# Attention, a dense expert and a soft mixture of experts on one core: another order of the first part

## The chip, the cores and the metric

The kernel is one program on one core of a Trainium2 chip. The metric is the time of one execution on the device in microseconds (us). The kernel before takes 650.18 us, the median of 3 runs (649.59 to 650.78).

## The reference, cut to what matters

Three parts follow each other: attention over chunks of 32 tokens with memory tokens, a dense layer with a squared ReLU, and a soft mixture of 8 experts. The change lies in the first two, where the attention of the first block of tokens and the first steps of the dense layer overlap.

```
for c in range(nc):                       # attention, chunk by chunk
    scores = scale * np.matmul(q_c, k_full.transpose(0, 1, 3, 2))
    scores = scores - np.max(scores, axis=-1, keepdims=True)
    a = np.exp(scores)
    a = a / (np.sum(a, axis=-1, keepdims=True) + 1e-09)
    out[:, :, c_start:c_end] = np.matmul(a, v_full)
...
h = x @ w_in                              # dense layer, 512 -> 2048 -> 512
r = np.maximum(h, 0.0)
g = s * (r * r) + b
return (g @ w_out).astype(np.float32)
...                                       # then the soft mixture on its result
```

## The kernel before, in words

The 3072 tokens are handled in 6 blocks of 512. In a block, the attention works on 4 pairs of heads, called units; the dense layer walks over 16 slices of 128 hidden columns, called steps. Blocks of the first pass are u = 0 to 3, the second block's are u = 4 to 7. Products in full precision are made of three fast matmuls: every operand is split into a high part and a low part, and high x high, high x low and low x high are summed. The weights of the dense layer arrive as raw 64-bit numbers and have to be turned into 32-bit floats first, half a slice at a time.

What is done, and by which engine, in the letters of the order that is written out by hand in the string FIRST (a letter and a number; the number is the unit, the step or the half slice):

- S and s spread q (L205, L207); B the scores on TensorE (L220); a the row maximum and the subtraction on VectorE (L234, L235); b the exponential on ScalarE (L239); f the sums and their reciprocals on VectorE (L247 to L249); j the scaling on GpSimd (L253).
- U is four transposes of a unit's probabilities on TensorE (L263). The result is copied into a block layout in two halves, p for the first (ScalarE, L273) and C for the second (VectorE, L275, or ScalarE, L273, by a list of units in the step table). V is the product with the values on TensorE (L285), u the copy of the high part of x on ScalarE (L292), X the low part of x on VectorE (L308).
- w loads half slices of weights into free staging tiles (L320, SyncE). d clamps (L326, VectorE for the halves 0 and 1, GpSimd for the others), e and h are the high and the low word (L330, L335, ScalarE), E merges them into the weight (L340, VectorE) and gives the staging tile back.
- I and i are the high and the low part of the first weight of a step (L347 ScalarE; L351 VectorE or GpSimd, by a list in wi_low), O and o those of the second weight (L362, L366).
- M is a step's first product, four quarters of three matmuls, one quarter for each unit's x (L377). For step 0 the quarters stand alone: H0 to H3. R is the ReLU (L381, ScalarE), t the square (L385, VectorE), g and l the high and low part of the result (L388 ScalarE, L392 VectorE). Y is the second product, 12 matmuls (L407).
- z is a group of multiplications of zeros that keeps TensorE busy (L1239), y puts six tiles into the list of staging tiles.

Every engine takes its own part of this order strictly one after the other, and waits by semaphore for what it reads and for buffers that must be free. H0 to H3 add into one bank of PSUM, which R0 reads when all four are done. M1 adds into another bank.

Of the kernel before, what the change touches and what calls it, by code (L numbers as in the profile page):

```python
# [12 lines left out]
ALU = mybir.AluOpType  # L13
# [4 lines left out]
NF = 16  # L18
# [7 lines left out]
KG = 40  # L26
KW = CB * KG + 24
FIRST = (
# [25 lines left out]
def tile_attention_moe_softmoe(  # L54
# [13 lines left out]
    pe, act, dve, pool, sp = nc.tensor, nc.scalar, nc.vector, nc.gpsimd, nc.sync  # L68
# [82 lines left out]
    def r32(ap):  # L151
        return ap.bitcast(F32R)
# [4 lines left out]
    def hl(t):  # L157
        return t.rearrange("p (a n) -> p a n", a=2)
# [10 lines left out]
    def qv(u):  # L169
        return Q[u % 2].rearrange("p (c h n) -> p c h n", h=2, c=CB)  # L170
# [12 lines left out]
    def pbv(u):  # L183
        return PB[u % 2].rearrange("p (i a h z n) -> p i a h z n", i=4, a=2, h=2, z=2)
# [84 lines left out]
    def att_half(u, b, z, fast=True):  # L269
        src = b.rearrange("p (i a h n) -> p i a h n", i=4, a=2, h=2)[64 * z:64 * z + 64]  # L270
        dst = pbv(u)[64 * z:64 * z + 64, :, :, :, z, :]
        if fast:
            act.activation(out=dst, in_=src, func=AF.Copy)  # L273
        else:
            dve.tensor_copy(dst, src)  # L275
# [12 lines left out]
    def att_copy(u, b):  # L288
        j, hp = jh(u)
        xt = hl(X[j % 2][hp])  # L290
        if j < NPL:
            act.activation(out=r32(xt[:, 0]), in_=b, func=AF.Copy)  # L292
        else:
            act.activation(out=xraw(j, hp), in_=b, func=AF.Copy)
# [53 lines left out]

    def wi_low(n):
        t, raw = hl(WI[n % 2]), W[n % NF][:, 0:512]  # L350
        (dve if n < NF and n not in (0,) else pool).tensor_tensor(out=r32(t[:, 1]), in0=raw, in1=t[:, 0], op=ALU.subtract)  # L351

    def split_wi(n):
        wi_high(n)
        wi_low(n)
# [869 lines left out]
    with tc.manual_schedule(engines={mybir.EngineType.PE, mybir.EngineType.SP}):  # L1225
# [15 lines left out]
        for i in range(2):  # L1241
            t = qv(i)
            pool.memset(t[0:64, :, 1, :], 0.0)
            pool.memset(t[64:128, :, 0, :], 0.0)
        for i in range(2):
            t = pbv(i)
# [3 lines left out]
        sbk = {}  # L1250
# [3 lines left out]
        def took(u, b=None):  # L1254
# [15 lines left out]
            "E": w_end,  # L1270
            "I": wi_high,
            "i": wi_low,
            "H": lambda kt: mm_h(0, (kt,)),
            "R": make_r,
# [13 lines left out]
            "f": att_sum,  # L1288
            "j": lambda u: att_mul(u, pool),
            "p": lambda u: att_half(u, sbk[u], 0),  # L1290
            "C": lambda u: att_half(u, sbk[u], 1, u in (0,)),
            "u": lambda u: att_copy(u, sbk[u]),
            "X": lambda u: att_low(u, sbk[u]),
            "Z": w_store,
# [330 lines left out]
```

## Time and profile before

| | |
|---|---|
| median of 3 runs | 650.18 us (649.59 to 650.78) |
| the profiled execution | 650.11 us, of which 648.3 us are the span that the profile shows |
| TensorE busy | 636.6 us (98%), 4965 matmuls |
| VectorE, ScalarE, GpSimd busy | 438.1, 352.7 and 272.5 us |
| mean granted clock of TensorE | 0.997 of full speed |

The profile is one execution. Times in it count from its first instruction. PE is TensorE, DVE is VectorE, ACT is ScalarE, POOL is GpSimd, SP is SyncE. A row of a timeline gives start, duration, engine, line, operation, result and operands; in brackets stands how long the engine was idle before it, and who ended that. Instructions that follow each other on an engine overlap somewhat, so the distance from one start to the next, here called a slot, is shorter than a duration. TensorE's clock has two levels: a granted clock of 1.00 is 2.4 GHz, 0.50 is 1.2 GHz.

### The profile page before, as it was taken

The numbers are of one execution on the slowest core, as the hardware profiler recorded it, in microseconds if no ns is written. First come the engines' busy times: TensorE is split into PE (matmuls) and PEld (weight loads), VectorE is DVE, ScalarE is ACT, GpSimd is POOL, SyncE is SP. The second block draws the span as 40 slices with busy tenths as digits, with TensorE's granted clock in tenths as the row PEclk, the third lists the DMA queues.
The fourth block names the chain that finished last, engine by engine and source line by source line (L and its number), as shares of the span: only waits on it lengthen the run. The fifth ranks groups of instructions, "written<-read, shape, count | busy, mean of one in ns | idle before, by whom it ended". The sixth has DMA issues, their size and how long they took to land.

```text
span 648.3 us, 12864 instructions
## 1 busy us (share of the span) xinstructions
PE 636.6 (98%) x4965; PEld 511.4 (79%) x4965; DVE 438.1 (68%) x716; ACT 352.7 (54%) x632; POOL 272.5 (42%) x219
## 2 busy tenths in 40 slices
PE   8999999999999999999999999999999999999995
PEld 7788888888878888888788887888887888886384
DVE  6999989666864678656566586616766879666233
ACT  5898787655555556554344555425644456454232
POOL 5897856343343584543534102454455516000000
PEclk9999999999999999999999999999999999999998
DMA  9998854576746755978854696469999789999998
GB/s 335 406 405 304 308 193 167 175 274 234 271 166 221 277 208 211 329 259 297 293 186 178 216 332 197 182 216 355 329 352 317 240 294 328 390 391 409 406 408 317
DMA packets 60109, 184.38 MB, mean 284 GB/s; under 512 B 6672, under 2 KB 6928, under 8 KB 60048
## 3 DMA queue, kind: packets, MB, share of 16 engines
q1 hardware_dynamic: 60048, 183.56, 77.7%
q8 instruction: 39, 0.64, 0.4%
q14 instruction: 22, 0.18, 0.1%
HBM read 137.40 MB, written 46.14 MB: 283 GB/s over the span
## 4 chain that ended last, share of the span: by engine, by line
PE 94%; DVE 2%; DMA 2%; ACT 1%; issue 0%; DVEq 0%; POOL 0%; SPq 0%; ACTq 0%; POOLq 0%
PE bank L407 28%; PE bank L737 24%; PE bank L377 13%; PE bank L995 12%; PE bank L285 3%; PE bank L220 3%; PE bank L1439 2%; PE bank L459 2%; PE bank L263 2%; PE bank L1480 1%; DMA out<-x03n 1%; PE bank L433 1%; PE bank L475 1%; DMA out<-epn 1%; PE bank L1239 1%; PE bank L513 0%
## 5 line engine op out<-in xcount | busy, mean ns | idle before, releaser
L407 PE MATMUL bank<-g,wo 128*128 128x512 f32 x528 | 130.0, 395 | 0.0
L407 PEld LDWEIGHTS bank<-g,wo 128*128 128x128 f32 x528 | 96.9, 188 | 21.7 <-ACT wi L347 0.8
L377 PE MATMUL bank<-x,wi 128*128 128x512 f32 x384 | 92.7, 390 | 0.0
L377 PEld LDWEIGHTS bank<-x,wi 128*128 128x128 f32 x384 | 71.8, 188 | 15.3 <-DVE x L308 0.4
L385 DVE SCALAR_TENSOR_TENSOR rt<-bank,cons,rt 128x512 f32<-128x512 f32 x32 | 23.9, 746 | 29.1 <-ACT rt L381 28.9
L326 POOL TENSOR_SCALAR sp<-sp 128x512 f32<-128x512 f32 x20 | 43.0, 2176 | 0.0
L366 POOL TENSOR_TENSOR wo<-w,wo 128x512 fp32r<-128x512 f32 x16 | 21.9, 1367 | 45.6 <-ACT wo L362 37.0
L729 POOL TENSOR_TENSOR w14n<-sp6n,w14n 128x512 fp32r<-128x512 f32 x8 | 14.5, 1815 | 46.9 <-ACT w14n L728 46.9
L351 POOL TENSOR_TENSOR wi<-w,wi 128x512 fp32r<-128x512 f32 x17 | 22.4, 1317 | 24.6 <-ACT wi L347 21.5
L347 ACT ACTIVATE wi<-w 128x512 fp32r<-128x512 f32 x32 | 20.1, 629 | 19.6 <-PE bank L377 14.8
L392 DVE SCALAR_TENSOR_TENSOR g<-rt,cons,g 128x512 fp32r<-128x512 f32 x32 | 25.6, 799 | 6.2 <-ACT g L388 5.9
L362 ACT ACTIVATE wo<-w 128x512 fp32r<-128x512 f32 x32 | 20.1, 628 | 16.8 <-PE bank L407 8.5
L285 PEld LDWEIGHTS bank<-pb,v 128*64 128x64 f32 x704 | 22.2, 138 | 8.0 <-issue 2.5
L388 ACT ACTIVATE g<-rt,cons 128x512 fp32r<-128x512 f32 x32 | 23.1, 722 | 9.0 <-DVE rt L385 8.7
L239 ACT ACTIVATE ep<-ep 128x512 f32<-128x512 f32 x22 | 13.9, 632 | 22.8 <-DVE ep L235 22.7
L285 PE MATMUL bank<-pb,v 128*64 128x64 f32 x704 | 25.1, 225 | 0.8 <-ACT pb L273 0.5
L220 PE MATMUL bank<-k,q 128*64 128x64 f32 x704 | 24.6, 225 | 0.3 <-DMA k<-kd 0.3
L752 ACT ACTIVATE rt1n<-y1n 128x1024 f32<-128x1024 f32 x8 | 8.5, 1058 | 29.0 <-DVE y1n L854 29.0
L220 PEld LDWEIGHTS bank<-k,q 128*64 128x64 f32 x704 | 22.6, 140 | 1.7 <-issue 1.3
L381 ACT ACTIVATE rt<-bank 128x512 f32<-128x512 f32 x32 | 18.7, 584 | 6.2 <-PE bank L377 6.1
L985 POOL TENSOR_TENSOR k0n<-sp5n,k0n 128x512 fp32r<-128x512 f32 x6 | 8.2, 1360 | 32.1 <-ACT k0n L984 32.1
L247 DVE TENSOR_REDUCE ast<-ep 128x8 f32<-128x512 f32 x22 | 15.0, 681 | 8.6 <-ACT ep L239 8.2
(688 smaller groups left out, 1727.5 us busy)
## 6 DMA issues: line engine op xcount, KB each, us to landing
v<-vd SPq DMA_DIRECT2D x22, 512.0 KB, 5.2
sp<-wd SPq DMA_DIRECT2D x22, 512.0 KB, 9.4
q<-qd SPq DMA_DIRECT2D x20, 512.0 KB, 7.5
dws<-wo SPq DMA_DIRECT2D x16, 512.0 KB, 6.2
k<-kd SPq DMA_DIRECT2D x22, 332.0 KB, 6.8
wo<-dws SPq DMA_DIRECT2D x12, 512.0 KB, 5.0
dwi<-w SPq DMA_DIRECT2D x16, 256.0 KB, 6.8
dwr<-w SPq DMA_DIRECT2D x16, 256.0 KB, 6.6
```

The costliest lines, as they stand in the source:

```text
L220: pe.matmul(S[64 * par:64 * par + 64, 2 * i + z, :], lhsT=qt[:, c].rearrange("p h n -> p (h n)"), rhs=kt[:, KG * c:KG * c + 64], start=Tru ...
L285: pe.matmul(b[64 * h:64 * h + 64, 64 * m:64 * m + 64], lhsT=vt[:, m, h, :], rhs=pb[:, m // 2, m % 2, h].rearrange("p z n -> p (z n)"), sta ...
L326: eng.tensor_scalar(out=hv, in0=hv, scalar1=-EXP_TOP, scalar2=EXP_TOP, op0=ALU.max, op1=ALU.min)
L351: (dve if n < NF and n not in (0,) else pool).tensor_tensor(out=r32(t[:, 1]), in0=raw, in1=t[:, 0], op=ALU.subtract)
L366: (dve if n < NF else pool).tensor_tensor(out=r32(t[:, :, 1]), in0=raw, in1=t[:, :, 0], op=ALU.subtract)
L377: pe.matmul(HB[n % 2], lhsT=r32(w[:, a, kt, :]), rhs=r32(x[:, b]), start=(kt == 0 and i == 0), stop=(kt == 3 and i == 2))
L385: dve.scalar_tensor_tensor(out=t, in0=HB[n % 2], scalar=s_col, in1=r, op0=ALU.mult, op1=ALU.mult)
L388: act.activation(out=r32(hl(G[n % 2])[:, 0]), in_=hl(RT[n % 2])[:, 1], func=AF.Identity, bias=b_col)
L392: dve.scalar_tensor_tensor(out=r32(g[:, 1]), in0=t, scalar=b_col, in1=g[:, 0], op0=ALU.add, op1=ALU.subtract)
L407: pe.matmul(yb[dt], lhsT=r32(w[:, dt // 2, a, dt % 2 * 128:dt % 2 * 128 + 128]), rhs=r32(g[:, b]), start=(first and i == 0), stop=(last an ...
L737: pe.matmul(b, lhsT=r32(wv[:, a, kt, :]), rhs=r32(xv[:, c]), start=(first and kt == 0 and i == 0), stop=(kt == 1 and i == 2), skip_group_c ...
L995: pe.matmul(banks[d], lhsT=r32(w[:, a, d * 128:d * 128 + 128]), rhs=r32(g[:, b]), start=(first and i == 0), stop=(last and i == 2), skip_g ...
```

## The change

The string FIRST is rewritten in its first five lines: the same 475 entries, some at other places. In the step table the list of units whose second copy is made by ScalarE grows from unit 0 to units 0, 1 and 3. In wi_low the low part for step 3 goes from VectorE to GpSimd. Nothing else is changed, and nothing that is computed.

```diff
 FIRST = (
...
-    "I1 e2 H3 i1 M1 E2 R0 d4 h3 t0 w1 O0 g0 o0 e3 d5 l0 Y0 R1 E3 h4 t1 w1 I2 d6 e4 i2 g1 E4 M2 h5 l1 w1 "
...
+    "v4 v5 X3 e2 i1 E2 M1 h3 H3 R0 t0 w1 d6 O0 g0 o0 e3 l0 h4 Y0 E3 R1 w1 I2 t1 e4 g1 h5 i2 E4 M2 l1 w1 "
...
     def wi_low(n):
         t, raw = hl(WI[n % 2]), W[n % NF][:, 0:512]
-        (dve if n < NF and n not in (0,) else pool).tensor_tensor(out=r32(t[:, 1]), in0=raw, in1=t[:, 0], op=ALU.subtract)
+        (dve if n < NF and n not in (0, 3) else pool).tensor_tensor(out=r32(t[:, 1]), in0=raw, in1=t[:, 0], op=ALU.subtract)
...
             "p": lambda u: att_half(u, sbk[u], 0),
-            "C": lambda u: att_half(u, sbk[u], 1, u in (0,)),
+            "C": lambda u: att_half(u, sbk[u], 1, u in (0, 1, 3)),
```

On TensorE the place is the end of the first block's attention and the first products of the dense layer. bank_195 takes H0 to H3, bank_196 takes M1; x_87 to x_90 are the four quarters of x; the row of pb_106 with yt_108 is V3, and the row of L407 is the start of Y0.

```order
 L377 MATMUL bank_195<-x_87,wi_83 128x512 x3
 L285 MATMUL bank_191<-pb_106,yt_108 64x64 x16
+L377 MATMUL bank_195<-x_89,wi_83 128x512 x3
 L377 MATMUL bank_195<-x_88,wi_83 128x512 x3
-L377 MATMUL bank_195<-x_89,wi_83 128x512 x3
-L377 MATMUL bank_195<-x_90,wi_83 128x512 x3
 L377 MATMUL bank_196<-x_87,wi_84 128x512 x3
 L377 MATMUL bank_196<-x_88,wi_84 128x512 x3
 L377 MATMUL bank_196<-x_89,wi_84 128x512 x3
 L377 MATMUL bank_196<-x_90,wi_84 128x512 x3
+L377 MATMUL bank_195<-x_90,wi_83 128x512 x3
 L407 MATMUL bank_191<-g_95,wo_85 128x512
```

H2 stands before H1, and H3 stands behind all of M1, directly in front of Y0. Ahead of that place, two of the multiplications of zeros have moved from before U0 to behind it.

On VectorE the place is the stretch from the end of the sums of the first block (RECIPROCAL) to the low parts of x. The copies of pb_106 are C1 and C3, the one of pb_105 is C2; w_67 is the merge E0, sp_113 the clamp d1.

```order
 L249 RECIPROCAL ast_188<-ast_188 128x8
-L275 COPY pb_106<-bank_192 64x16x32
 L340 SCALAR_TENSOR_TENSOR w_67<-sp_112 128x512
 L275 COPY pb_105<-bank_193 64x16x32
+L326 TENSOR_SCALAR sp_113<-sp_113 128x512
 L308 TENSOR_TENSOR x_87<-bank_191,x_87 128x512
-L326 TENSOR_SCALAR sp_113<-sp_113 128x512
-L275 COPY pb_106<-bank_197 64x16x32
 L308 TENSOR_TENSOR x_88<-bank_194,x_88 128x512
```

C1 and C3 are gone from VectorE, and d1 stands before X0 in place of behind it.

On ScalarE the place is the same stretch, from the copies of the last unit on. The copies of pb_106 are p3 and, new, C3; x_89 and x_90 are u2 and u3; L335 is the low word h, L330 the high word e, and wi_84 is I1.

```order
 L273 ACTIVATE pb_106<-bank_197 64x16x32
 L335 ACTIVATE sp_113<-sp_113 128x512
+L273 ACTIVATE pb_106<-bank_197 64x16x32
 L292 ACTIVATE x_89<-bank_198 128x512
 L330 ACTIVATE sp_113<-sp_113 128x512
+L292 ACTIVATE x_90<-bank_191 128x512
 L335 ACTIVATE sp_114<-sp_114 128x512
-L292 ACTIVATE x_90<-bank_191 128x512
 L347 ACTIVATE wi_84<-w_68 128x512
```

C3 stands between h1 and u2, and u3 stands before h2. C1 has come in further ahead, behind e0 (not shown). On GpSimd, i3 stands behind the clamp d8, which now comes before d7. Since E1 now comes after y0, its staging tile is loaded again as the fourth of a group and not as the second.

## Rows read from the trace of the kernel before

**Rows 1.** The page: costliest groups, busy us, mean ns, then idle before them

```profile
L407 PE MATMUL bank<-g,wo 128*128 128x512 f32 x528 | 130.0, 395 | 0.0
...
L377 PE MATMUL bank<-x,wi 128*128 128x512 f32 x384 | 92.7, 390 | 0.0
```

**Rows 2.** The chain of waits, 17 to 40 us: start, us, what

```profile
21.39 0.70 DVE pb L275
...
22.14 1.15 PE bank L285 x32
23.29 5.22 PE bank L377 x21
...
31.30 2.72 PE bank L377 x12
```

**Rows 3.** Timeline of VectorE, 10 to 80 us: C1, E0, d1, E1, i1, t0

```profile
17.34 0.69 DVE L275 COPY pb<-bank 64x512 f32<-64x512 f32 x1
18.06 0.98 DVE L340 SCALAR_TENSOR_TENSOR w<-sp 128x512 uint32<-128x512 uint32 x1
...
20.41 0.95 DVE L326 TENSOR_SCALAR sp<-sp 128x512 f32<-128x512 f32 x1
...
23.32 1.05 DVE L340 SCALAR_TENSOR_TENSOR w<-sp 128x512 uint32<-128x512 uint32 x1
...
25.07 0.69 DVE L351 TENSOR_TENSOR wi<-w,wi 128x512 fp32r<-128x512 f32 x1
...
26.74 0.74 DVE L385 SCALAR_TENSOR_TENSOR rt<-bank,cons,rt 128x512 f32<-128x512 f32 x1
```

**Rows 4.** Timeline of ScalarE: e0, p2, p3, h1, u2, e1, u3, R0, g0, I3

```profile
16.48 0.66 ACT L330 ACTIVATE sp<-sp 128x512 f32<-128x512 f32 x1
17.85 0.59 ACT L273 ACTIVATE pb<-bank 64x512 f32<-64x512 f32 x1 [0.71 <-PE bank L263]
...
20.09 0.58 ACT L273 ACTIVATE pb<-bank 64x512 f32<-64x512 f32 x1
20.57 0.67 ACT L335 ACTIVATE sp<-sp 128x512 uint32<-128x512 uint8 x1
21.13 0.57 ACT L292 ACTIVATE x<-bank 128x512 fp32r<-128x512 f32 x1
21.61 0.63 ACT L330 ACTIVATE sp<-sp 128x512 f32<-128x512 f32 x1
...
23.34 0.60 ACT L292 ACTIVATE x<-bank 128x512 fp32r<-128x512 f32 x1 [0.52 <-PE bank L285]
...
25.80 0.60 ACT L381 ACTIVATE rt<-bank 128x512 f32<-128x512 f32 x1 [0.19 <-PE bank L377]
...
27.51 0.72 ACT L388 ACTIVATE g<-rt,cons 128x512 fp32r<-128x512 f32 x1
...
34.38 0.61 ACT L347 ACTIVATE wi<-w 128x512 fp32r<-128x512 f32 x1
```

**Rows 5.** Timeline of GpSimd: j3 and i0

```profile
17.45 1.04 POOL L253 TENSOR_TENSOR rt<-rt,ast 128x512 f32<-128x512 f32 x1 [0.41 <-DVE ast L249]
19.78 1.29 POOL L351 TENSOR_TENSOR wi<-w,wi 128x512 fp32r<-128x512 f32 x1 [1.29 <-ACT wi L347]
```

**Rows 6.** Timeline of TensorE: keep-warm passes at the start and later, and U2

```profile
1.31 3.79 PE L1239 MATMUL bank<-w 128*128 128x128 f32 x16 [1.31 <-POOL w L1235]
...
12.50 1.06 PE L1239 MATMUL bank<-w 128*128 128x128 f32 x8
...
17.09 0.65 PE L263 MATMUL bank<-cons,rt 128*128 128x128 f32 x4 [0.17 <-POOL rt L253]
```

**Rows 7.** Transfers issued from 8.4 to 8.8 us: KB, us to landing

```profile
sp<-wd SPq DMA_DIRECT2D x1, 512.0 KB, 10.5
```

**Rows 8.** Stretches at the end: us, busy PE, PEld, DVE, ACT, POOL, granted clock, DMA, GB/s

```profile
642.00:643.00 1.00, 0.23 (x1) 0.00 (x0) 1.00 (x3) 0.67 (x2) 0.00 (x0) 1.00 0.74 293
643.00:644.00 1.00, 0.00 (x0) 0.00 (x0) 0.21 (x1) 0.00 (x0) 0.00 (x0) 1.00 1.00 381
644.00:645.00 1.00, 0.00 (x0) 0.00 (x0) 0.00 (x0) 0.00 (x0) 0.00 (x0) 0.61 1.00 383
```

8 rows, old and new, of the table FIRST are left out of this document.

## The prediction

> **What bounds the kernel now.** I read the costliest groups of the page first. The two big matmul groups, L407 with 528 and L377 with 384 instructions, show 0.0 us of idle time in front of them [rows 1]. From its first full product on, TensorE therefore waits for nobody, and whatever moves the start of that stream moves the end by the same amount. I then followed the chain of waits through the stretch in which the stream begins [rows 2]. Before 22.14 us the chain runs on VectorE, whose last link is the copy L275 of the fourth head pair's probabilities (21.39 us, 0.70). From 22.14 on every link is TensorE: the value product V3 (1.15 us), then one piece of 21 matmuls (5.22 us) that contains H1, H2, H3 and M1, and then blocks of 12 in 2.72 us, or 0.227 us for one matmul. The third view is the timelines of the engines in that stretch [rows 3 to 6]: they give what one instruction takes, the distance from one start to the next on ScalarE, and how long a result of TensorE needs before ScalarE starts on it.
>
> One more thing has to be seen there. The first Y product needs R0, t0 and g0 in a row, and R0 needs all four quarter products H0 to H3. R0 starts at 25.80, t0 at 26.74, g0 at 27.51 and ends at 28.23 [rows 3, 4]. TensorE spends just that time on the 12 matmuls of M1 (12 x 0.227 = 2.72 us), so the latency is covered. The cover is M1, and it works only because M1 stands behind H3.
>
> **The change part by part.**
>
> *Two probability copies go to ScalarE.* VectorE loses two copies of 0.70 us [rows 2, 3]. ScalarE takes each in a form of 0.59 us (17.85) whose slot costs 0.48, by the starts 20.09 and 20.57 [rows 4]. C1 follows the exponent step at 16.48, which takes 0.66, so it ends near 17.7 and V1 starts there; with V3's 1.15 us as its length it ends at 18.85. U3 comes next, 0.65 us by the row at 17.09 [rows 6], and its result reaches ScalarE 0.76 us after its start (17.09 to 17.85) [rows 4, 6], which is 19.6. ScalarE then does p3 (slot 0.48), h1 (slot 0.56, from 20.57 to 21.13) and C3 (0.59): C3 ends near 21.2, and V3 starts at 21.25. Before it was 22.14, so this part brings 0.9 us at V3.
>
> *The clamp and the merge.* The clamp d1 moves ahead of X0 on VectorE. Its data is issued at 8.41 us and lands 10.5 us later [rows 7], at 18.9, about when the copy C2 is done, so no new wait is expected of it. It took 0.95 us beside GpSimd's subtraction at 19.78 [rows 3, 5]. Even at that price X0 is done before 21, and V3 behind it still waits for C3. The merge E1 (1.05 us at 23.32 [rows 3]) needs e1. With u2 in the slot behind C3 (21.1) and e1 0.48 later for 0.63 us [rows 4], E1 runs from about 22.4 to 23.4. Because E1 frees its staging tile after the other tiles are listed, SyncE fetches that tile as the fourth of a group and not as the second. I cost this at nothing: GpSimd's queue of clamps lies between landing and use. Were that cover gone, it would be one clamp late, in a part of the program with no idle in front of TensorE.
>
> *Keep-warm multiplications.* Two move behind U0. TensorE waits there for others anyway; cost 0.
>
> *i3 to GpSimd.* The subtraction takes 1.29 us there (19.78) in place of 0.69 (25.07) [rows 3, 5]. I3 starts at 34.38 [rows 4]; with the delay of R0 found below (2.2 us) its 0.61 us ends at 37.2, and i3 at 38.5. M3 is three blocks after Y0, and its third matmul, the first one that needs i3, comes at about 30.2 + 3 x 2.72 + 0.45 = 38.8. So it is hidden by 0.3 us. Without that cover the cost would be about 0.3 us, and at least 0.
>
> *The quarter products.* This is the term that decides. The order is now H2, H1, M1, H3.
> First M1 has to start. V3 at 21.25 gives u3 at 22.45 (1.20 us, from 22.14 to 23.34 [rows 2, 4]); u3 holds a slot of 0.48 and h2 one of 0.56: I1 starts at 23.5 and ends at 24.1; i1 (0.69) ends at 24.8. H2 and H1 are done by 23.8. The third matmul of M1 needs i1, so from 24.85 on 10 matmuls of M1 and the 3 of H3 are left: 13 x 0.227 = 2.95 us, to 27.8. The last one, 0.39 us long [rows 1], ends near 28.0.
> Then nothing is left for TensorE to do. R0 runs 28.0 to 28.6 (0.60), t0 to 29.37 (0.74 and 0.03 between engines), g0 to 30.12 (0.72 and 0.03). Y0 cannot start before, where g0 ended at 28.23. That is 1.9 us later, with TensorE idle for almost 2.4 us, in spite of the 0.9 us won at V3.
>
> **Bounds.** Above: E0 now starts at 17.34, where C1 stood, just ahead of j3 on GpSimd (17.45, 1.04 us) [rows 3, 5]. E0 took 0.98 us beside the end of j3, so the two hinder each other. If j3 is the one that waits, and for the whole of E0, it ends at 19.4 in place of 18.5, U3 and all behind it come 0.5 late, and the sum is 2.4 us. The Trainium skill, "SBUF — State Buffer", section "Who interferes with whom", says that VectorE with two SBUF inputs and a GpSimd instruction that reads SBUF take a shared pair of ports in turn, the first of them for its whole instruction; by that rule j3 is held, and the sum is the 2.4 of the bound in place of 1.9. The trace agrees at d1 (20.41 to 21.36), which ends 0.29 us after GpSimd's 19.78 + 1.29 = 21.07, and shows no case with VectorE first. Below: if no wait at all were left behind U2 (17.09), TensorE's own work would be two transposes (1.30), three value products (3.45) and 24 matmuls (5.45), ending at 27.3; R0, t0, g0 with their handovers add 2.15, and Y0 starts near 29.5, 1.2 us later than the g0 end of before allowed. I take 2.0, since the steps on ScalarE are rows in the same order and only j3 is open. 650.11 us, of which 648.3 are span, become 652.1; the median of the runs shown, 650.18, becomes 652.2.
>
> **Rivals.**
> The gap also costs clock. In the last microseconds TensorE does its last 0.23 us of work after 642.00, and the granted clock is still 1.00 (2.4 GHz) in 643 and 0.61 on average in the microsecond from 644 [rows 8]: it fell to the 1.2 GHz level some 2 us after the last matmul. A gap of 2.4 us, with another short wait for i1 shortly ahead, is of that size; against it speaks that TensorE is much busier before this gap than in the tail. The price from rows: at the start 16 warm-up passes took 3.79 us, where 8 later took 1.06, so 16 should take 2.12; 1.67 us were lost in a slow stretch [rows 6]. Part of such a stretch would fall into the gap itself, so I take 1.5 on top of 2.0: 653.7. The Trainium skill, "TensorE: Matmul & The Clock Gate", section "HAM oscillation — how this bites in real kernels", warns of just this, idle gaps that put the engine back to the lower clock so that the next products start slow; the tail agrees with it, and no gap of this size in the middle of this trace tests it.
>
> Everything keeps up. If the copies on ScalarE free the start of the stream so far that I1 and i1 are no longer waited for, only the bound below is left, 1.2 us, and 651.4 is no measurable change. For it speaks that VectorE is the chain up to V3 and gets lighter. Against it speaks that V3 still waits for C3, now behind U3, p3 and h1 on ScalarE, and M1 for I1. It decides from the point where V3 starts before about 20.6.
>
> The other side: the delay is given back, as other engines gain 2 us of lead on TensorE and later waits vanish, and with V3 0.9 us earlier the kernel gets faster by some of that, at most 649.3. Against it: there are no waits of TensorE in front of the two large groups to be saved [rows 1]. It would need H3 to be done by 25.8 us as before, which 24.85 for i1 excludes.
>
> **How the numbers follow.** What a measurement of this kernel can tell from no change is about 0.2%, 1.3 us. Chances: forecast 0.58, with its own range 651.6 to 652.9; clock as well 0.27; everything keeps up 0.11; given back 0.04. The first two are slower, 0.85; the third is the same, 0.11; the last is faster, 0.04. The range, 651.2 to 654.2, takes in the bound below at one end and the clock at the other.
>
> **What would show it.** Right: in the profile after, V3 near 21.3; TensorE's block at L407 first starts near 30.2, with an idle time of more than 2 us in front of it that ends with ScalarE's L388; L381 first starts near 28.0; and from then on the stream has the shift of 2 us up to the end. The copies L275 at C1 and C3 stand on ScalarE in slots of 0.48. The clock rival shows as a granted clock under 1.00 around 28 to 34 us and matmuls of twice 0.227. Wrong: an L407 that starts before 29.6, or a shift at the end that differs from that at 30 us by more than 0.5.

## The result, and the profile after

The changed kernel takes 655.94 us, the median of 5 runs (655.55 to 656.24); the kernel before takes 650.18 (649.59 to 650.79, 5 runs). The ratio is 1.0082, with a 95% interval of 1.0071 to 1.0092: slower by 5.8 us, where 2.0 were forecast and 654.2 was the upper end of the range. The profiled execution took 655.63 us, of which 653.8 are the span: 5.5 more than before.

On the page, the group L407 now has idle time in front of it, where it had none [rows 1]. Columns as there.

```profile
L407 PE MATMUL bank<-g,wo 128*128 128x512 f32 x528 | 131.6, 399 | 3.0 <-ACT g L388 3.0
...
L377 PE MATMUL bank<-x,wi 128*128 128x512 f32 x384 | 93.4, 391 | 0.5 <-DVE x L308 0.3
```

The timeline of TensorE shows where these 3.0 us stand: one gap of 2.28 us in front of Y0, as forecast, and a second one of 0.72 us at 84 us, which nothing in the forecast explains.

```profile
21.17 0.73 PE L377 MATMUL bank<-x,wi 128*128 128x512 f32 x2 [0.32 <-DVE x L308]
21.84 1.15 PE L285 MATMUL bank<-pb,yt 128*64 128x64 f32 x32
...
24.76 3.97 PE L377 MATMUL bank<-x,wi 128*128 128x512 f32 x15 [0.20 <-ACT wi L347]
31.01 4.60 PE L407 MATMUL bank<-g,wo 128*128 128x512 f32 x12 [2.28 <-ACT g L388]
...
84.03 3.01 PE L407 MATMUL bank<-g,wo 128*128 128x512 f32 x12 [0.72 <-ACT g L388]
```

The first Y0 block takes 4.60 us where a block at full clock takes about 3.0. The stretches of one microsecond (columns as in [rows 8]) show the granted clock fall behind the gap, to 0.50 or 1.2 GHz, and come back at 35 us.

```profile
31.00:32.00 1.00, 0.99 (x4) 0.80 (x5) 1.00 (x2) 1.00 (x3) 1.00 (x2) 0.84 1.03 410
32.00:33.00 1.00, 1.00 (x4) 0.81 (x3) 1.00 (x2) 0.72 (x3) 1.00 (x1) 0.50 1.01 401
...
35.00:36.00 1.00, 1.00 (x6) 0.83 (x5) 0.51 (x1) 1.00 (x3) 0.00 (x0) 0.95 0.99 389
```

The chain of waits from 15 to 90 us is the view that shows the surprise. Before, it ran on TensorE from 22.14 us on [rows 2]. Now it runs over GpSimd, ScalarE and VectorE (and one transfer that SyncE issues behind them) up to 84.03 us, and TensorE comes into it only there.

```profile
20.54 10.28 POOL sp L326 x5
31.10 2.52 POOL yt L326
33.62 4.71 issue
38.37 1.30 POOL wi L351
39.67 2.41 POOL yt L326
42.10 0.66 ACT yt L330
...
81.28 1.28 DVE w L340 x2
82.56 0.67 DVE rt L385
83.26 0.73 ACT g L388
84.03 3.01 PE bank L407 x12
```

On VectorE the rows to see are d1 and X0 ahead of V3, the long wait for t0, the wait of the merge E6 at 38.88, and instructions with two inputs that last 0.97 us and more where others of the same line last 0.69 [rows 3]. (The name behind the arrow at 29.45 is misleading: t0 needs R0, which ends at 29.36.)

```profile
18.27 0.69 DVE L275 COPY pb<-bank 64x512 f32<-64x512 f32 x1 [0.61 <-ACT pb L273]
19.20 1.20 DVE L326 TENSOR_SCALAR sp<-sp 128x512 f32<-128x512 f32 x1 [0.24 <-DMA sp<-wd]
20.43 1.29 DVE L308 TENSOR_TENSOR x<-bank,x 128x512 fp32r<-128x512 f32 x2
...
29.45 0.75 DVE L385 SCALAR_TENSOR_TENSOR rt<-bank,cons,rt 128x512 f32<-128x512 f32 x1 [2.96 <-POOL sp L326]
...
38.88 1.34 DVE L340 SCALAR_TENSOR_TENSOR w<-sp 128x512 uint32<-128x512 uint32 x1 [1.25 <-ACT sp L335]
...
49.28 1.12 DVE L340 SCALAR_TENSOR_TENSOR w<-sp 128x512 uint32<-128x512 uint32 x1
...
51.38 0.97 DVE L351 TENSOR_TENSOR wi<-w,wi 128x512 fp32r<-128x512 f32 x1
```

On ScalarE: R0, which came at 25.80 before [rows 4]; then I3, with the low word h6 behind it; then the high word e7, which waits for GpSimd.

```profile
28.76 0.60 ACT L381 ACTIVATE rt<-bank 128x512 f32<-128x512 f32 x1 [2.93 <-PE bank L377]
...
37.66 0.63 ACT L347 ACTIVATE wi<-w 128x512 fp32r<-128x512 f32 x1 [0.23 <-DVE w L340]
38.20 0.65 ACT L335 ACTIVATE sp<-sp 128x512 uint32<-128x512 uint8 x1
...
42.10 0.66 ACT L330 ACTIVATE yt<-yt 128x512 f32<-128x512 f32 x1 [0.46 <-POOL yt L326]
```

On GpSimd, i3 stands 4.75 us waiting for I3, and the clamp d7 stands behind it.

```profile
31.10 2.52 POOL L326 TENSOR_SCALAR yt<-yt 128x512 f32<-128x512 f32 x1
38.37 1.30 POOL L351 TENSOR_TENSOR wi<-w,wi 128x512 fp32r<-128x512 f32 x1 [4.75 <-ACT wi L347]
39.63 2.44 POOL L326 TENSOR_SCALAR yt<-yt 128x512 f32<-128x512 f32 x1
```

From these timelines one can read, block by block, how much later than before the same instruction starts. t0, t2, t3, t4 and t8 are the squares L385 on VectorE, Y0, Y1 and Y8 the blocks L407 on TensorE (before: t0 26.74, t8 76.84, Y0 28.35, Y1 33.86, Y8 78.68). The last two columns are the median less that of the kernel before in the same comparison, and the ratio's interval. One profiled execution stands for each row, and the start of the stream varies between executions: e1, e13 and e14, described below, have the same order up to Y0, and it starts at 31.29, 32.03 and 31.71 us. So what a column gains or loses against an earlier one of its row says more than a difference of some tenths between two rows.

| kernel, us late | t0 | t2 | t3 | t4 | t8 | Y0 | Y1 | Y8 | median | interval of the ratio |
|---|---|---|---|---|---|---|---|---|---|---|
| changed kernel | 2.71 | 4.03 | 4.83 | 5.61 | 5.64 | 2.66 | 4.33 | 5.35 | +5.8 | 1.0071 to 1.0092 |
| e1 only H3 late | 2.91 | 3.23 | 3.23 | 4.06 | 4.09 | 2.94 | 3.15 | 3.80 | +4.0 | 1.0055 to 1.0082 |
| e4 changed, H3 early | | 0.95 | 1.77 | 2.54 | 2.56 | 0.00 | | 2.27 | +2.9 | 1.0037 to 1.0063 |
| e3 changed, i3 on VectorE | | 3.34 | 3.90 | | 4.71 | 2.91 | 4.57 | 4.57 | +4.5 | 1.0060 to 1.0084 |
| e5 both undone | -0.19 | 0.57 | 0.53 | 1.37 | 1.39 | -0.23 | 0.47 | 1.10 | +1.0 | 1.0007 to 1.0024 |
| e9 changed, d7 first | 2.70 | 3.67 | 3.68 | 3.69 | 3.69 | 2.65 | 4.35 | 4.35 | +4.0 | 1.0048 to 1.0073 |
| e6 only the copies | -0.28 | -0.48 | -0.70 | -0.56 | -0.59 | -0.13 | -0.17 | -0.17 | -0.8 | 0.9985 to 1.0003 |

From Y8 on, the shift stays constant through the middle of the program. Before, g8 ended at 78.34 and Y8 started at 78.68, so VectorE and ScalarE could be 0.3 us later without TensorE noticing: the shift at Y8 is the larger of TensorE's own (at Y7) and that of t8 less 0.3. In the profiles of all 16 altered kernels this comes out within 0.02 us. In the last stage, behind 615 us, single executions then gain or lose up to some 1.5 us more; a difference of one microsecond is therefore read from the shift at Y8 and the median together.

### The profile page after: what moved, and what is told of

It is laid out like the page before. It is cut to its first block, busy times and chain, and to the rows that moved or that the text cites. A ratio compares the mean times of both kernels' runs of the same rounds, so it can differ in the third digit from the quotient of the medians.

```text
span 653.8 us, 12864 instructions
## 1 busy us (share of the span) xinstructions
PE 638.3 (98%) x4965; PEld 511.4 (78%) x4965; DVE 438.0 (67%) x713; ACT 353.8 (54%) x634; POOL 273.9 (42%) x220
## 4 chain that ended last, share of the span: by engine, by line
PE 83%; DVE 4%; DMA 4%; POOL 3%; ACT 2%; issue 2%; SPq 1%; DVEq 0%; ACTq 0%; POOLq 0%
PE bank L407 24%; PE bank L737 23%; PE bank L995 11%; PE bank L377 9%; PE bank L285 3%; PE bank L220 2%; PE bank L1439 2%; PE bank L1480 2%; DMA sp<-wd 2%; PE bank L459 2%; POOL sp L326 2%; PE bank L263 1%; DMA q<-qd 1%; DVE w L340 1%; PE bank L475 1%
## 5 line engine op out<-in xcount | busy, mean ns | idle before, releaser
L407 PE MATMUL bank<-g,wo 128*128 128x512 f32 x528 | 131.6, 399 | 3.0 <-ACT g L388 3.0
L407 PEld LDWEIGHTS bank<-g,wo 128*128 128x128 f32 x528 | 98.1, 190 | 25.6 <-ACT g L388 3.7
L385 DVE SCALAR_TENSOR_TENSOR rt<-bank,cons,rt 128x512 f32<-128x512 f32 x32 | 23.9, 746 | 31.7 <-ACT rt L381 28.6
```

What stands on the lines that cost most here:

```text
L385: dve.scalar_tensor_tensor(out=t, in0=HB[n % 2], scalar=s_col, in1=r, op0=ALU.mult, op1=ALU.mult)
L407: pe.matmul(yb[dt], lhsT=r32(w[:, dt // 2, a, dt % 2 * 128:dt % 2 * 128 + 128]), rhs=r32(g[:, b]), start=(first and i == 0), stop=(last an ...
```

## The experiments

**H3 behind M1, alone and undone.** e1 is the kernel before with one move, e4 the changed kernel with H3 moved back.

```
e1  -"I1 e2 H3 i1 M1 E2 R0 ...      e4  -... E2 M1 h3 H3 R0 ...
    +"I1 e2 i1 M1 H3 E2 R0 ...          +... E2 H3 M1 h3 R0 ...
```

> The kernel before with one entry moved: H3 behind M1 on TensorE, all other engines' orders the same. Theory A (two losses that add up: R0 late by the quarter order, and i3 in front of d7 in GpSimd's queue): M1's third matmul still waits for i1 until 25.8, then 13 matmuls of 0.227, R0 near 29.0, Y0 near 31.2, and t0 to t8 on VectorE all late by the same 2.7 to 3.0 us; total 652.9 to 653.3, up to 654.8 where the clock falls in the gap and nothing absorbs it. Theory B (all of the 5.7 us comes from H3 behind M1, as VectorE and ScalarE stand still behind R0 and never catch up): 655 to 656, with t8 more than 5 us late.

> The changed kernel with H3 moved back ahead of M1, everything else as changed. Theory A: no gap before Y0 and no fall of the clock; i3 still waits for I3 on GpSimd in front of d7, which makes e7 and E7 late and VectorE late by 1 to 3 us at t8: 651 to 653. Theory B: 649.2 to 650.3, as fast as the kernel before or faster by what the copies on ScalarE bring.

e1 took 654.52 us, +4.0; the gap in front of Y0 was 2.37 us. e4 took 653.36 us, 0.4 more than theory A gave, with t8 2.56 late as it had it: Y0 was not late at all, and TensorE had no gap and no fall of the clock there. The step costs about 3 us where it stands: Y0 2.94 and t0 2.91 late in e1, and from V3 to Y0 it is 9.29 us in e1 and 6.21 before, a distance without the variation of the start. The shift at Y8 is 3.80 us with it alone and 3.08 of the changed kernel's. Neither theory for e1 fits: t8 is 4.09 us late, less than B and more than A, and the time is A's for a fallen clock although the clock stayed at 1.00 in its profile. Most of what A had missed is 0.8 us between t3 and t4, taken up below. What follows: the quarter products are the largest cause, at least half of the loss. But e4 is still 2.9 us late, though TensorE's start is on time, so another engine makes the rest.

**i3 on GpSimd, alone and undone.** In wi_low, e2 gives i3 to GpSimd in the kernel before, e3 gives it back to VectorE in the changed one.

```
e2  -... not in (0,) else pool) ...       e3  -... not in (0, 3) else pool) ...
    +... not in (0, 3) else pool) ...         +... not in (0,) else pool) ...
```

> The kernel before with i3 on GpSimd in place of VectorE, behind d8 where d7 is already done. Theory A: i3 starts after d8 at 36.4 and ends at 37.7, M3's third matmul comes 0.7 us late, d9 and the clamps behind it 1.3 us later with idle time of GpSimd at 50 us to take that up: 650.5 to 651.4. Theory B: i3 is hidden, 650.2 plus or minus 0.3.

> The changed kernel with i3 back on VectorE, so that d7 follows d8 on GpSimd without a wait for I3. Theory A: only the lateness of R0 is left, t0 to t8 are all late by 2.7 to 3.1 us, no second gap of TensorE near 84 us: 652.8 to 653.3, up to 654.6 in executions in which the clock falls in the gap before Y0. Theory B: no difference from the changed kernel, 655.9.

e2 took 652.07 us, +1.6 (ratio 1.0015 to 1.0032), more than either theory gave; there M3 itself waits, by the row of TensorE's timeline that follows. e3 took 654.94 us; t8 is 0.9 us and Y8 0.8 us earlier than in the changed kernel. The second gap of TensorE is gone, but t0 to t8 are not equally late, as theory A had it: 1.75 us are added from 2.96 to 4.71. Of these, 0.50 stand in front of t3, which waits for R3 and so for a TensorE delayed by the fallen clock, and 0.85 between t3 and t4.

```profile
38.09 2.56 PE L377 MATMUL bank<-x,wi 128*128 128x512 f32 x10 [0.97 <-POOL wi L351]
```

So i3 on GpSimd is no free move: it costs about 1 us in either kernel. In e2 the wait is that of M3, the consumer that the forecast looked at; in the changed kernel M3 has no wait, and the cost comes on another way.

**Both undone.** e5 is the changed kernel with the edits of e3 and e4.

> The changed kernel with both taken back: H3 ahead of M1 and i3 on VectorE. What is left of the change is the copies on ScalarE and the order of the clamps, merges and words. Theory A (VectorE is the second bound, full from 26 to 85 us with less than 1 us of idle time, so each idle stretch that the new order gives it stays): h6 behind I3 still makes VectorE wait some 1.2 us for E6, so t8 comes 1 to 1.7 us late and the time is 651.0 to 652.0. Theory B (the remaining edits cost nothing and the copies bring what was predicted at V3): 649.5 to 650.4.

e5 took 651.88 us (ratio 1.0007 to 1.0024), as theory A had it: the two steps are most of the loss, and 1.0 us is left over.

**d7 ahead of i3.** e9 keeps the changed kernel's i3, but GpSimd clamps d7 before d8 and i3.

```
-... t1 e4 g1 h5 i2 E4 M2 ... g2 d7 e7 ...
+... t1 e4 g1 h5 i2 E4 d7 M2 ... g2 e7 ...
```

> The changed kernel with d7 ahead of d8 and i3 on GpSimd, so that the wait of i3 for I3 no longer holds d7 back. Theory A: e7 and e8 on ScalarE and E7 and E8 on VectorE come without their waits (0.37 and 0.42 us), t3 and t8 0.8 to 1.3 us earlier, 654.7 to 655.2. Rival (the wait of i3 costs nothing, only the place of H3 does): 655.9.

e9 took 654.81 us, as theory A had it. VectorE's waits for e7 (0.37 and 0.42 us) are gone and t3 is 1.15 us earlier than in the changed kernel. This is a price of i3 that the forecast did not see: not M3, but the clamp queued behind it. t8 is even 1.95 us earlier, since between t3 and t4 VectorE needs 8.20 us, as before (8.19), and not 8.97.

**Taking work off VectorE.** e6 is the kernel before with only the copies C1 and C3 on ScalarE; e7 also gives C4 and C5 of the changed kernel to ScalarE; e11 leaves C4 and C5 out (that part of the result is left out).

```
e6  -... u in (0,))      e7  -... u in (0, 1, 3))          e11 -att_half(u, sbk[u], 1, ...)
    +... u in (0, 1, 3))     +... u in (0, 1, 3, 4, 5))        +None if u in (4, 5) else att_half(...)
```

> The kernel before with only C1 and C3 moved to ScalarE. V3 starts 0.5 to 0.9 us earlier. Theory A: ScalarE's queue (u3, I1, e2, R0 each a slot later) takes most of it back, Y0 starts within 0.4 us of 28.35, and the time is 649.8 to 650.7. Rival: the 0.9 us at V3 goes through to the end, 649.3 to 649.7.

> The changed kernel with two more copies of VectorE, C4 and C5 (0.69 us each, near 62 and 67 us), on ScalarE, far behind the place of the change. Theory A: VectorE is what makes the second product of step 8 late, so t8 comes 1.0 to 1.4 us earlier and TensorE's gap near 84 us goes: 654.6 to 655.0. Theory B (TensorE's own gap at 28 us and the clock make the time): no difference, 655.6 to 656.2.

> After without the second halves of the probability copies of units 4 and 5 (that part of the result is left out); VectorE loses two instructions of 0.7 us and ScalarE gets nothing. Theory, that the end is set by VectorE and ScalarE together, both without slack: ScalarE loses nothing, but the part of the delay that VectorE alone holds goes; t8 comes 0.6 to 1.4 us earlier than in the changed kernel, 654.6 to 655.4 us. Rival, that ScalarE alone sets it: 655.9 us, unchanged. Rival, that TensorE's own late start sets it: 655.9 us as well, with t8 earlier.

e6 took 650.05 us, a ratio of 0.9985 to 1.0003: no difference that can be told. t8 gains 0.6 us, but Y8 only 0.2, as TensorE's own start gains no more. e7 took 656.83: no gain, t8 5.57 late; VectorE now stands waiting for ScalarE in five places of 0.39 to 0.68 us. That missed the expectation and says that ScalarE has no room there. e11 took 655.42 us, where the theory gave up to 655.4; t8 is 4.73 and Y8 4.44 late, 0.9 less than in the changed kernel. Counted from t0 of the same execution t8 is 1.39 us earlier, just what the two copies last, so what is taken from VectorE there comes out at t8 in full. So VectorE and ScalarE together are a second bound beside TensorE.

**The clock.** e12 is e9 with eight multiplications of zeros in the gap (16 instructions in the trace).

```
-... M1 h3 H3 R0 ...
+... M1 h3 H3 x8 R0 ...
```

> The kernel with d7 moved ahead of d8 and i3 (654.81 us, Y1 4.35 us late with the fall of the clock, no second gap) and, in the gap of TensorE between H3 and Y0, eight multiplications of zeros (added work). Theory, that there the fall of the clock is what sets the end: granted clock stays at 1.00, Y1 is 2.7 us late, and the end is then set by t8, 3.7 us late, less 0.3: 653.8 to 654.2 us. Rival, that the fall is absorbed: 654.8 us.

The timeline of TensorE shows the filled gap and a Y0 of full speed; the granted clock is 1.00 throughout.

```profile
28.73 1.95 PE L1294 MATMUL bank<-w 128*128 128x128 f32 x16
31.17 3.01 PE L407 MATMUL bank<-g,wo 128*128 128x512 f32 x12 [0.50 <-ACT g L388]
```

Y1 is 2.88 us late in place of 4.35, and Y8 3.52 in place of 4.35. So in e9 the fall did set the shift at Y8, by 0.8 us. The time does not show it, and the theory's range is missed: 656.86 us, with two executions at 655.02 and 655.17 and three from 656.86 to 657.19, more than e9's. In the profiled execution (655.17) the gain is lost in the last stage, in one wait of TensorE that the profile ascribes to nothing, by the chain of waits:

```profile
631.25 1.44 PE bank L1480 x47
632.69 1.91 issue
634.60 0.27 PE bank L1480
```

Why that wait arises, and whether it makes the three longer executions, stays open. Other kernels show the fall in their times, if one goes by the mean granted clock of each execution: in e1 the one execution with 0.995 took 656.35 us and the five with 0.997 to 0.999 took 653.86 to 654.89; in e13, which follows, two with 0.995 took 654.96 and 655.78, three with 0.997 and 0.998 took 653.91 to 654.63.

**What slows VectorE between t3 and t4.** With H3 late alone, this interval is 0.8 us longer than before, without idle time. e13 is e1 without the clamps d10 to d14 on GpSimd (that clamp is left out); e10 is e5 with h6 ahead of I3 on ScalarE; e14 and e15 are e1 and e5 with the merge E10 of VectorE behind the row maximum a5.

```
e13 "d": lambda k: None if 10 <= k <= 14 else w_clamp(k)
e10 -... E5 d8 I3 i3 Y1 h6 w1 ...        e14, e15 -"E10 a5 w1 O4 ...
    +... E5 d8 h6 I3 i3 Y1 w1 ...                 +"a5 E10 w1 O4 ...
```

> Before with H3 behind M1 (654.52 us; t3 3.23 and t4 4.06 us late) and without the clamps of the half slices 10 to 14 on GpSimd (that clamp is left out). Theory, that the 0.8 us between t3 and t4 are VectorE's merges and low parts slowed by GpSimd's clamps beside them: t4 and t8 are at most 3.3 us late and the end is set by TensorE's own 3.15: 653.4 to 653.9 us. Rival, that the clamps have no part in it: t4 4.0 us late and 654.5 us.

> After with H3 ahead of M1, i3 on VectorE and, beside that, the low word h6 ahead of I3 on ScalarE (with H3 and i3 alone: 651.88 us, E6 waited for h6 and t2 was 0.57 us late). Theory, that what is left of the loss is this wait of the full VectorE: the wait of E6 goes, t2 is within 0.15 us of before, t8 at most 0.8 us late, 650.4 to 651.2 us. Rival, that what is left comes from something else (phase of VectorE against GpSimd): 651.7 to 652.1 us.

> The kernel before with H3 behind M1, and in it the merge E10 of VectorE (1.53 us beside GpSimd's scaling j4, 0.69 in the kernel before) moved behind the row maximum a5, so that it starts after j4 has ended. With H3 alone: t3 3.23 and t4 4.06 us late, 654.52 us. Theory, that the 0.8 us between t3 and t4 are this one merge, held up by the scaling: it takes 0.7 to 0.8 us, t4 and t8 are 3.2 to 3.4 us late, Y8 at most 3.2, about 653.8 us. Rival, that VectorE loses the time there anyhow (with the next clamp, for instance): t4 4.0 us late and 654.5 us.

> The changed kernel with H3 ahead of M1, i3 on VectorE (651.88 us, t3 0.53, t4 1.37, Y8 1.10 us late) and E10 moved behind a5. Theory, that the merge beside the scaling is 0.84 us of what these two steps leave: t4 and t8 at most 0.6 us late, Y8 0.5 us, 651.0 to 651.3 us. Rival: t4 1.4 us late, 651.9 us.

e13 took 654.63 us, about what the rival gave, and the interval stayed at 9.03 us, though GpSimd had nothing to do for 12.66 us. (t4 is 5.54 us late there, but t0 is so by 3.64 already.) So the theory of the clamps fell for this place. Its timeline shows the culprit, a single merge of 1.53 us which starts 0.33 us after GpSimd's scaling:

```profile
51.02 1.31 POOL L253 TENSOR_TENSOR ep<-ep,ast 128x512 f32<-128x512 f32 x1 [12.66 <-DVE ast L249]
51.35 1.53 DVE L340 SCALAR_TENSOR_TENSOR w<-sp 128x512 uint32<-128x512 uint32 x1
```

Before, GpSimd was still in a clamp when the sums were ready; the scaling started at 46.95, and the merge, at 46.66, was ahead of it and took 0.69. e1, e3, e5, e10, e13 and e16 have the scaling first (1.53 or 1.54 us for the merge); the kernel before, e6, e9 and e12 have the merge first (0.68 or 0.69). In the changed kernel, e2, e4, e7 and e11 the loss falls on two other instructions beside clamps (1.12 to 1.14 and 0.96 to 0.98).

e14 and e15 confirm the duration and miss the time. By e14's timeline the merge takes 0.68 us behind a5, but now O4 on ScalarE waits for it, R4 stands behind O4, and t4 waits for R4:

```profile
51.99 0.68 DVE L340 SCALAR_TENSOR_TENSOR w<-sp 128x512 uint32<-128x512 uint32 x1
...
52.78 0.63 ACT L362 ACTIVATE wo<-w 128x512 fp32r<-128x512 f32 x1 [1.70 <-DVE w L340]
...
53.32 0.58 ACT L381 ACTIVATE rt<-bank 128x512 f32<-128x512 f32 x1
...
53.93 0.75 DVE L385 SCALAR_TENSOR_TENSOR rt<-bank,cons,rt 128x512 f32<-128x512 f32 x1 [1.27 <-ACT rt L381]
```

From t3 to t4 it is now 9.52 us in e14, against 9.02 in e1, and 9.53 in e15, against 9.03 in e5. e14 takes 655.63 us (ratio 1.0063 to 1.0087), e15 652.87 (1.0024 to 1.0048). The experiment made the mistake that it was to explain: it moved an instruction without asking who stands behind its result. e10 took 652.41 us, more than theory and rival gave, and brought nothing: the wait before t2 moved from the merge to i3 (0.85 us, for I3), since ScalarE works without a pause from 30.4 to 36.5 us there. Of the last 1.0 us of e5, the slow merge (0.84 us between t3 and t4) is seen in rows; that it alone makes them is not shown, since no run removed it without a new wait.

**A version faster than both?** e16 is e6 with C3 ahead of h1 on ScalarE.

```
-... p3 d1 h1 C3 ...
+... p3 d1 C3 h1 ...
```

> The kernel before with the copies C1 and C3 on ScalarE (650.05 us beside 650.86) and C3 ahead of h1 there. Looked for is a version faster than both. Theory, that V3 waits for C3, C3 for h1 in front of it, and that TensorE has no idle time from V3 on: V3 0.5 us earlier than with the copies alone (21.4 to 21.5), Y0 27.7, t8 0.6 us early as there, the end 0.5 us earlier than before, about 650.0 us where before has 650.5. Rival, that I1 and i1, half a slot later by h1, now make M1 wait: Y0 28.1 to 28.3, 650.5 us.

V3 starts at 21.48 and Y0 at 28.05, 0.3 us earlier than before, but the merge E10 comes behind the scaling (1.53 us), and t8 is 1.22, Y8 0.93 us late. e16 took 650.83 us, a ratio of 0.9994 to 1.0013: no difference. No version beat the kernel before.

## Why the prediction was wrong

**What bounds the kernel.** "From its first full product on, TensorE therefore waits for nobody, and whatever moves the start of that stream moves the end by the same amount" is the step that failed. The first half is what the rows said; the second does not follow. VectorE had 0.5 us of waits between 26 and 58 us before, ScalarE works in turn with it, and their slack against TensorE at Y8 was 0.3 us. Rows of the kernel before show it: the two waits of VectorE, and g8 and Y8.

```profile
32.83 0.80 DVE L366 TENSOR_TENSOR wo<-w,wo 128x512 fp32r<-128x512 f32 x1 [0.25 <-ACT wo L362]
...
34.51 1.08 DVE L340 SCALAR_TENSOR_TENSOR w<-sp 128x512 uint32<-128x512 uint32 x1 [0.28 <-ACT sp L330]
```

```profile
77.61 0.73 ACT L388 ACTIVATE g<-rt,cons 128x512 fp32r<-128x512 f32 x1 [1.17 <-DVE rt L385]
```

```profile
78.68 3.02 PE L407 MATMUL bank<-g,wo 128*128 128x512 f32 x12
```

A delay that hit them, or a wait put among them, was made up by t8 in no run with H3 late. The shift grew from 2.66 us at Y0 to 5.35 at Y8, far beyond the 0.5 that the prediction named as its refutation.

**The quarter products.** The mechanism was right: Y0 behind a gap of 2.28 us, ended by g0, against almost 2.4 forecast. The size at Y0 was 2.66 us in place of 1.9 to 2.0. Most of the missing 0.7 came from ahead of V3, next point. Not seen was that the same 2.9 us of waiting stand on ScalarE (2.93 in front of R0) and on VectorE (2.96 in front of t0). VectorE had almost no idle time to give, and three of ScalarE's four waits of 0.23 us and more in that stretch before were for VectorE.

**The copies and the clamp.** V3 was forecast for 21.25 us and came at 21.84, 0.3 and not 0.9 us earlier than before. C3 was in time, at 20.63; what was late was X0, at 20.43, behind the clamp d1, which waited 0.24 us for its transfer and took 1.20. The two matmuls of H0 that stand behind this wait take from 21.17 to V3. "V3 behind it still waits for C3" forgot that H0 stands between them on TensorE; the clamp, costed at nothing, cost 0.6 us by these rows. e6 bears this out, as it has the copies on ScalarE but d1 behind X0. There V3 starts 4.38 us after U2; in the changed kernel it is 4.95, before it was 5.05, and the forecast had 4.16. So the part brought 0.1 and not 0.9 us, and the other 0.2 at V3 are the earlier start of that execution. U2 and V3 in e6, and U2 in the changed kernel:

```profile
17.57 0.66 PE L263 MATMUL bank<-cons,rt 128*128 128x128 f32 x4 [0.17 <-POOL rt L253]
...
21.95 1.15 PE L285 MATMUL bank<-pb,yt 128*64 128x64 f32 x32
```

```profile
16.89 0.66 PE L263 MATMUL bank<-cons,rt 128*128 128x128 f32 x4 [0.17 <-POOL rt L253]
```

The upper bound, j3 held for the whole of E0, did not come about: E0 was first, at 17.02 us for 0.64, and had 0.4 us left when j3 came at 17.25; j3 took 1.31 us in place of 1.04, 0.3 more.

**i3 on GpSimd.** "Hidden by 0.3 us" was worked out for M3 alone. In e2 even M3 waited 0.97 us. In the changed kernel the price came through VectorE's merges: 0.8 us up to t2, where e3 needs 6.61 us from t1 and the changed kernel 7.43, and 0.8 up to t3, where VectorE waits for e7 and e7 for d7, by e9 (4.69 and 5.48 us from t2). The sum over t8's shift of 5.64 is: 2.71 at t0; 0.22 up to t1; 1.10 up to t2, where E6 waits 1.25 us for h6 and then takes 1.34 beside i3 (0.28 and 1.08 before); 0.80 up to t3, the waits behind d7; 0.78 up to t4, two instructions of 1.12 and 0.97 us beside clamps; 0.03 after that.

**The clock.** The rival given 0.27 happened, with 1.65 us at Y0 against 1.5 forecast. But it is not part of the sum in the changed kernel: Y1 is 4.33 us late with it, and the other chain alone gives 5.35 at Y8. The times say the same: the profiled execution, with a mean granted clock of 0.994, and a second one with 0.995 took 655.63 and 655.55 us; the three with 0.998 and 0.999 had no such fall (over the stretches above it takes 1.7 us off the clock, or 0.003 off the mean) and took 655.94, 656.24 and 655.94. Where TensorE's own shift sets the end, as at Y8 in e9, it counts.

**The other rivals.** That the other engines gain lead on TensorE is refuted by t8, which in every kernel with H3 late is later than Y0 was: they lose more. That everything keeps up is refuted by the gap.

## What to carry to other kernels

An engine with no idle time in front of it is not the only bound: look how much lead the engines that feed it have where it is smallest, and whether they have idle time to win it back; if not, a delay on their side is kept as well, and the end goes by the larger of the two shifts. For every instruction that is moved, ask first who waits for it, and then what stands behind it on its new engine and behind those who wait.

## What was not expected of the hardware

A merge of VectorE, which reads both of its inputs from SBUF, took 1.53 us in place of 0.69 when GpSimd's scaling (1.31 us) had started 0.3 us before it, ending 0.5 to 0.6 us after the scaling, as if it did its work only behind it. This agrees with the rule that the prediction named, the Trainium skill, "SBUF — State Buffer", section "Who interferes with whom". Beside GpSimd's clamps, which last 2.0 to 2.5 us each and follow each other without a pause, the same instructions took 0.97 to 1.17 us if they started up to 0.6 us after a clamp did, as at 49.28 after 48.77 and at 51.38 after 51.15 in the changed kernel, and mostly 0.69 if they started later in it. So a clamp does not hold VectorE for its whole length, which that rule would have it do. (The profile gives GpSimd's spans only roughly.) Which of these cases an instruction meets depends on the phase of the two engines: a shift of some tenths of a microsecond upstream made 0.8 us in the interval from t3 to t4.

The same gap in front of Y0 does not always cost clock: with 2.28 us the granted clock fell to 0.50 in the profiled executions of the changed kernel, of e3 and of e9, and stayed at 1.00 in those of e11 and, with 2.29, of e7; with 2.37 us it fell in e13 and not in e1 and e14, whose order is the same at that place.
